# New keys for the attention units' schedule: scores in 0.95 of a unit, transposed scores in 0.9

## The chip, the core and the metric

The kernel runs on one core of one Trainium2 chip. The core's engines work side by side, each through its own instructions in a fixed order: TensorE (PE, matmuls; its weight loads are shown as PEld), VectorE (DVE), ScalarE (ACT), GpSimd (POOL), and SyncE (SP), which issues most DMAs. The metric is the device time of one execution in microseconds, as the median of several runs.

## The reference

One transformer block on 2048 rows of 576 columns. A condition vector gives six modulation vectors (shift, scale and gate for each half). The first half is attention in 32 heads of 18 columns with a sliding window of 256 keys:

```python
q, k, v = qkv[0], qkv[1], qkv[2]
scores = jnp.einsum("bhqd,bhkd->bhqk", q, k) * (Dh ** -0.5)
mask = (idx[:, None] - idx[None, :] >= 0) & (idx[:, None] - idx[None, :] < W)
scores = jnp.where(mask[None, None], scores, -1e9)
p = _softmax(scores, axis=-1)
o = jnp.einsum("bhqk,bhkd->bhqd", p, v)
...
x = x + ga * _A_ref(h, A_wqkv, A_wo)
h = _layernorm(x, axis=-1) * (1 + cb) + sb
x = x + gb * _B_ref(h, B_w1, B_w2, B_w3, B_w4)
```

The second half, `_B_ref`, mixes rows by small shifts and applies an MLP with 4608 inner columns. All of it is in float32; the kernel reaches that accuracy by splitting operands into an upper and a lower half and summing three products.

## The kernel before

The kernel has three stages. `phase_a` is attention with its projections, `phase_b` the row mixing, `phase_c` the MLP. The change lies in `phase_a` alone.

**Units.** Queries come in 4 groups of 512 rows, heads in 8 packs of 4. That gives 32 *units*, u = 0 to 31, each for four heads of one group. A unit's work, by the functions that the listing below shows:

- `pack(u)` (SP) loads the unit's queries and keys from DRAM into one of three buffers `Q[u % 3]`, `K[u % 3]`, as nine DMAs (L494 queries, L497 keys); they may start when the unit three back has used the buffer for the last time.
- `scores(u)`: 16 score matmuls (`one`, L511; four row tiles by four heads) go into a ring of three PSUM banks. VectorE adds the mask and reduces each to its row maxima (`red`, L518). After the sixteenth, `neg` (VectorE, L524 and L525, 16 columns each) negates the maxima in two halves, `mt` transposes them on TensorE (L532), `ms` copies them on ScalarE (L537) and issues a small DMA from ScalarE's queue (L538), which puts them as two extra rows into the unit's queries.
- `attend(u)`: 12 transposed scores (`xs`, three bank layouts by four heads, each some matmuls of L558 and mask matmuls of L567) go into a ring of two PSUM banks; because of the extra rows the maxima are subtracted already. ScalarE takes the exponential (`ex`, L577). Then `av` multiplies by the values (48 matmuls of L588, or fewer in the first group), `cp` copies the result, `ot` transposes it (L599), `on` divides by the sums, and `store` writes it to DRAM.

**Between the units** stand the projections: `qk_item` (queries and keys of a group, 14 matmuls of 512 columns in 7 steps, L417, then copy, split and store) and `v_item` (values, 288 columns in 4 steps). Ahead of each group from the second on, the group's four row tiles are normalised (`x_norm`) and transposed (`x_tr`): TensorE transposes column block k into the bank `tr` or `mm` (L381), ScalarE scales it (`ev`, L389), GpSimd casts the upper half (`hi`, L392), and VectorE subtracts for the lower half (`lo`, L396). GpSimd also sums the later modulation vectors (`modvec`, L649, L651) and scales the output weights (L698). From unit 22 on `s4a` applies the output projection to finished row tiles: it loads a tile's attention rows and x, transposes them (L888), multiplies (L922), and normalises twice; the loads and the weights for the next stage join SP's queue.

**The order** is written out by hand. Each step is a pair of a *key* and a function; the keys count in units. All pairs are sorted by key and the functions called in that order (`play`), so every engine gets its instructions in the order of the keys. At run time nothing is reordered: a key is no time, only a place. In a stretch where fewer matmuls have keys TensorE goes through the keys faster. An engine whose next instruction waits holds back all behind it.

In `s4a`, `quiet` moves a load or store whose key has a fraction between 0.04 and 0.38 to the fraction 0.38, and `free` chooses PSUM banks that the bank `av` of the units does not use at that time. The class constants `win` (the keys between which each group's projections run), `o_p`, `o_x` and `o_a` are offsets of the packing, the transposed scores and the attend matmuls.

Of the kernel before, what the change touches and what calls it, by code (L numbers as in the profile page):

```python
# [53 lines left out]
class Kern:  # L54
# [132 lines left out]
    def phase_a(self):  # L187
# [10 lines left out]
        with ExitStack() as st:  # L198
# [40 lines left out]
            def vones(a, b):  # L239
                def f():  # L240
                    for v in V[a:b]:
                        nc.gpsimd.memset(v, 1.0)
                return f
# [128 lines left out]
            def x_tr(g, k, t0):  # L372
                n = P if k < KC else TAIL
                box = {}

                def tr():
                    if k == 0:
                        hT[g] = gp.tile([P, 2 * KC + 1, 512], F32R, tag="L", name=f"hT{g}", bufs=1)
                    pa = box["p"] = ps([P, 4, P], ("tr", "mm", "tr", "mm", "tr")[k], f"hT{g}_{k}")
                    for i in range(4):  # L380
                        nc.tensor.transpose(pa[:n, i, :], xrows[4 * g + i][:, k * P:k * P + n], self.ident)  # L381

                def ev():
                    if k % 2 == 0:
                        h0["t"] = kp.tile([P, 2, 512], F32, tag="qe", name=f"h{g}_{k}", bufs=2)
                    h = h0["t"][:, k % 2, :]
                    box["h"] = h
                    p = h0["p"][k] if g == 0 else box["p"]
                    nc.scalar.activation(h[:n], p[:n].rearrange("p a b -> p (a b)"), AF.Identity, bias=sa[:n, k:k + 1], scale=ca[:n, k:k + 1])  # L389

                def hi():
                    nc.gpsimd.tensor_copy(hT[g][:n, k if k < KC else 2 * KC, :], box["h"][:n])  # L392

                def lo():
                    o = hT[g][:, KC + k, :] if k < KC else hT[g][TAIL:, 2 * KC, :]
                    nc.vector.tensor_tensor(out=o, in0=box["h"][:n], in1=hT[g][:n, k if k < KC else 2 * KC, :].bitcast(F32), op=ALU.subtract)  # L396
                if g == 0:
                    b = -8.84 + 0.01 * k if k < KC else -8.79
                    return [(b, ev), (b + 0.001, hi), (b + 0.021, lo)]
                return [(t0, tr), (t0 + 0.02, ev), (t0 + 0.055, hi), (t0 + 0.105, lo)]  # L400

            def x_tr0(i):
                def f():
# [96 lines left out]
            def scores(u):  # L500
                g = u // NU
                q, k = Q[u % 3], K[u % 3]
                box, reds = [], {}

                def one(i, h):
                    def f():
                        if not box:
                            box.append(sm.tile([P, 4, 4], F32, tag="m", name=f"m{u}", bufs=2))
                        lo = 0 if g else max(0, 2 - i) * P
                        sc = ps([P, 3 * P], "sc", f"sc{u}_{i}_{h}")  # L510
                        nc.tensor.matmul(sc[:, lo:], q[0:2 * R3, h, i * P:(i + 1) * P], k[0:2 * R3, h // 2, i * P + lo:(i + 3) * P], start=True, stop=True)  # L511
                        reds[i, h] = sc, lo
                    return f

                def red(i, h):
                    def f():
                        sc, lo = reds[i, h]
                        nc.vector.tensor_tensor_reduce(out=sc[:, lo:], in0=sc[:, lo:], in1=mask[:, lo:], scale=1.0, scalar=-3e38, op0=ALU.add, op1=ALU.max, accum_out=box[0][:, i, h:h + 1])  # L518
                    return f

                def neg():
                    m = box[0]
                    mr = sm.tile([P, 4, 8], F32R, tag="mr", name=f"mr{u}", bufs=2)
                    nc.vector.scalar_tensor_tensor(out=mr[:, :, 0:4], in0=m, scalar=-1.0, in1=zeros, op0=ALU.mult, op1=ALU.add)  # L524
                    nc.vector.scalar_tensor_tensor(out=mr[:, :, 4:8], in0=m, scalar=-1.0, in1=mr[:, :, 0:4].bitcast(F32), op0=ALU.mult, op1=ALU.subtract)  # L525
                    box.append(mr)

                def mt():
                    mr = box[1]
                    pm = ps([8, 4, P], "av" if 0 < u < 23 else "tr", f"mT{u}", F32R)  # L530
                    for i in range(4):
                        nc.tensor.transpose(pm[:, i, :], mr[:, i, :], self.identr)  # L532
                    box.append(pm)

                def ms():
                    ms = kp.tile([8, 512], F32R, tag="avs", name=f"ms{u}", bufs=1)
                    nc.scalar.copy(ms, box[2].rearrange("p a b -> p (a b)"))  # L537
                    nc.scalar.dma_start(q[2 * R3:2 * R3 + 2, :, :].bitcast(F32), ms.bitcast(F32))  # L538
                e = []
                for n, (i, h) in enumerate((i, h) for i in range(4) for h in range(4)):  # L540
                    t = u - 1 + (n + 0.5) / 16
                    e += [(t, one(i, h)), (t + 0.02, red(i, h))]
                return e + [(u + 0.01, neg), (u + 0.13, mt), (u + 0.15, ms)]

            banks = [[(0, 0, 3, 1), (3, 3, 1, 0)], [(1, 1, 3, 0), (-2, 0, 1, 3)], [(-1, 0, 2, 0), (2, 2, 2, 2)]]
            low = [((0, 3, 1), (1, 0, 2)), ((1, 0, 1), (0, 2, 2)), ((None, 1, 2),)]
# [1 line left out]
            def attend(u):  # L548
# [5 lines left out]
                def xs(b, h):  # L554
                    def f():
                        x = ps([P, 512], "st", f"X{u}_{b}_{h}")
                        for n, (kb, q0, w, p0) in enumerate(bk[b]):
                            nc.tensor.matmul(x[:, p0 * P:(p0 + w) * P], k[0:2 * R3 + 2, h // 2, (kb + 2) * P:(kb + 3) * P], q[0:2 * R3 + 2, h, q0 * P:(q0 + w) * P], start=(n == 0), stop=False)  # L558
                        c0 = min(s[3] for s in bk[b])
                        c1 = max(s[3] + s[2] for s in bk[b])  # L560
                        ms = []
                        for m, p0, w in low[b]:
                            p0, w = max(p0, c0), min(p0 + w, c1) - max(p0, c0)
                            if w > 0:
                                ms.append((maskb[:, 2 - w:2] if m is None else maskb[:, m].unsqueeze(1).to_broadcast([P, w, P]), p0, w))
                        for n, (m, p0, w) in enumerate(ms):
                            nc.tensor.matmul(x[:, p0 * P:(p0 + w) * P], self.identb, m, start=False, stop=(n == len(ms) - 1))  # L567
                        X[b, h] = x, c0, c1
                    return f
# [10 lines left out]
                def av(b):  # L580
                    def f():
                        if not abox:
                            abox.append(ps([P, 512], "av", f"av{u}"))
                        for n, (kb, q0, w, p0) in enumerate(bk[b]):
                            v = V[(4 * g + kb) % 10]
                            for h in range(4):
                                hh = 4 * (u % NU) + h
                                nc.tensor.matmul(abox[0][32 * h:32 * h + 32, q0 * P:(q0 + w) * P], v[:, hh * VA:hh * VA + 32], Pt[b, h // 2][:, p0:p0 + w, h % 2, :], start=(b == 0 and n == 0), stop=(b == 2 and n == len(bk[b]) - 1))  # L588
                    return f
# [34 lines left out]
                e = []  # L624
                for b in range(3):
                    for h in range(4):
                        t = u + self.o_x + (4 * b + h + 0.5) / 12
                        e += [(t, xs(b, h)), (t + 0.015, ex(b, h))]
                    e.append((u + self.o_x + 1 + self.o_a - 0.001 * (2 - b), av(b)))
                t = u + self.o_x + 1 + self.o_a  # L630
                return e + [(t + 0.03, cp), (t + 0.152, ot), (t + 0.167, on), (t + (0.36 if u < NB * NU - 1 else 0.17), store)]

            def modvec(v):
# [76 lines left out]
            ev = [(-9.5, warm(36)), (-9.45, consts), (-9.44, vones(0, 4)), (-9.405, c_load), (-9.2, wm_load), (-9.05, cond)]  # L710
# [6 lines left out]
            for k in range(KC + 1):  # L717
                ev += x_tr(0, k, 0.0)
# [21 lines left out]
            for g in range(1, NB):  # L740
# [11 lines left out]
                t = w0  # L752
# [21 lines left out]
            for t in range(12):  # L774
                t0 = w1 + 0.12 + 0.72 * t
# [79 lines left out]
        self.lc = itertools.count()  # L855

    win = {1: (2.6, 9.25), 2: (9.7, 16.1), 3: (16.55, 22.73)}
    o_p, o_x, o_a = 1.6, 0.42, 0.18

    def s4a(self, t, kp):  # L860
        nc, gp, Wo = self.nc, self.gp, self.Wo
        base = self.win[NB - 1][1] + 0.12 + 0.72 * t

        def free(a, b):
            lo, hi = self.o_x + self.o_a - 0.08, self.o_x + self.o_a + 0.04
            return all((base + a - n > hi) or (base + b - n < lo) for n in range(int(base), int(base) + 3))
        if free(0.56, 0.785):
            kinds = "mm", "av", "av" if free(0.135, 0.2) else "mm"
# [75 lines left out]
        e = [(quiet(-0.6, -0.25), load_o), (quiet(-0.35, 0.2), load_x)]  # L944
# [627 lines left out]
```

## Time and profile before

| what | value |
|---|---|
| median of 3 runs | 1675.13 us (1673.27 to 1676.79) |
| profiled execution | 1673.19 us |
| its span, first to last instruction | 1671.4 us |
| busy share of PE, DVE, ACT, POOL | 98%, 70%, 43%, 49% |
| mean granted TensorE clock | 0.998 |

How to read the lines that follow. In a *timeline* a line is start in us, duration in us, engine, source line, operation, output tile, inputs, shapes and a count; in brackets the engine's idle time just before it and whose end released it. PE's matmuls overlap, so a matmul's duration is longer than the time to the next one's start. In a *table of waits* a line is who waited, for whom, and total us, number of waits, longest us. In the *table by stage* a line is the stretch, its length, the busy time (and count) of PE, PEld, DVE, ACT and POOL, the granted clock, the DMA engines' share and GB/s. L with a number is a line of the kernel before.

### The profile page before, as it was taken

To read this page: it belongs to the slowest core of one execution; us is meant where nothing else is said; L and a number is where in the kernel's file an instruction comes from. 1 tells how busy PE (TensorE), PEld (TensorE's weight loads), DVE (VectorE), ACT (ScalarE), POOL (GpSimd) and SP (SyncE) were. 2 spreads that over 40 slices of the span, in tenths; PEclk is the share of its full clock that TensorE was granted. 3 is DMA by queue.
4 is the path that set the end of the run, shared out by engine and by line. 5 is a ranking of instruction groups with operands and counts; after the bars stand their busy time and mean duration, and the time that the engine had idled before them with its cause. 6 is when DMAs were issued, how large, how long until landed. Compare 5 with 4: busy or idle time off the path is not lost.

```text
span 1671.4 us, 30559 instructions
## 1 busy us (share of the span) xinstructions
PE 1638.5 (98%) x11115; PEld 1423.2 (85%) x11115; DVE 1163.4 (70%) x2417; ACT 714.7 (43%) x1373; POOL 816.0 (49%) x833
## 2 busy tenths in 40 slices
PE   9999999999999999999999999999999999999999
PEld 5877788778777787889999999999999999999998
DVE  5765765666666774767788878888885666666667
ACT  3454554555546656444344434443424222222221
POOL 6432332232436552243478888888863333322335
PEclk9999999999999999999999999999999999999999
DMA  7654554545477756345356556555575454445443
GB/s 227 192 152 133 147 145 133 151 110 153 118 170 210 216 181 200 124 137 189 123 211 222 197 172 216 206 200 177 214 246 179 152 168 158 134 144 176 148 133 109
DMA packets 160190, 283.03 MB, mean 169 GB/s; under 512 B 37412, under 2 KB 76836, under 8 KB 160040
## 3 DMA queue, kind: packets, MB, share of 16 engines
q1 hardware_dynamic: 159720, 280.55, 54.2%
q8 instruction: 88, 1.44, 0.4%
q14 instruction: 62, 0.51, 0.1%
q10 hardware_dynamic: 320, 0.52, 0.1%
HBM read 168.71 MB, written 111.63 MB: 168 GB/s over the span
## 4 chain that ended last, share of the span: by engine, by line
PE 88%; DVE 4%; DMA 2%; POOL 2%; ACT 2%; issue 2%; SPq 0%; ACTq 0%; POOLq 0%; DVEq 0%
PE pall L1431 27%; PE pall L1477 24%; PE pall L417 9%; PE pall L588 5%; PE pall L558 4%; PE pall L511 4%; PE pall L834 3%; PE pall L567 3%; PE pall L1213 3%; PE pall L922 2%; DVE pall L518 1%; PE pall L973 1%; PE pall L599 1%; DMA Q<-ms 1%; DMA wm<-in_w_mod_dram 1%
## 5 line engine op out<-in xcount | busy, mean ns | idle before, releaser
L1477 PEld LDWEIGHTS pall<-W,G 128*128 128x128 f32 x3036 | 428.3, 188 | 19.2
L1477 PE MATMUL pall<-W,G 128*128 128x288 f32 x3036 | 440.6, 294 | 0.0
L518 DVE CUSTOM_DVE_ANT_0 pall<-pall,mask 128x384 f32<-128x384 f32 (+2 forms) x512 | 270.3, 544 | 174.1 <-PE pall L511 171.5
L1431 PE MATMUL pall<-LNT,W 128*128 128x512 f32 x1512 | 374.8, 390 | 0.0
L1486 DVE TENSOR_TENSOR accA<-pall,accA 128x576 f32<-128x576 f32 (+1 forms) x337 | 254.0, 755 | 120.8 <-PE pall L1477 109.2
L1402 POOL TENSOR_TENSOR g<-g,g 128x512 f32<-128x512 f32 x140 | 185.3, 1324 | 292.7 <-DVE G L1397 150.4
L1431 PEld LDWEIGHTS pall<-LNT,W 128*128 128x128 f32 x1512 | 274.7, 188 | 45.5
L577 ACT ACTIVATE P<-pall 128x512 f32<-128x512 f32 (+2 forms) x384 | 216.8, 571 | 153.8 <-PE pall L567 145.2
L1394 ACT CAST G<-g 128x512 fp32r<-128x512 f32 x249 | 151.1, 620 | 271.6 <-POOL g L1402 270.4
L1397 DVE TENSOR_TENSOR G<-g,G 128x512 fp32r<-128x512 f32 x249 | 240.7, 968 | 11.6 <-ACT G L1394 11.5
L1435 ACT ACTIVATE g<-pall 128x512 f32<-128x512 f32 x144 | 85.8, 596 | 194.6 <-PE pall L1431 185.0
L1486 DVE TENSOR_TENSOR accB<-pall,accB 128x576 f32<-128x576 f32 x134 | 101.3, 757 | 91.1 <-PE pall L1477 89.2
L417 PE MATMUL pall<-hT,Wc 128*128 128x512 f32 x504 | 161.3, 420 | 3.2 <-ACT Wc L322 1.9
L511 PE MATMUL pall<-K,Q 108*128 108x384 f32 (+2 forms) x352 | 125.3, 367 | 1.5 <-DVE m L518 1.3
L1431 PE MATMUL pall<-big,W 128*128 128x512 f32 x504 | 126.2, 390 | 0.0
L442 POOL CAST qe<-qe 128x512 fp32r<-128x512 f32 x36 | 22.6, 627 | 211.1 <-ACT qe L438 184.3
L567 PE MATMUL pall<-maskb,identb 128*128 128x256 bf16 (+1 forms) x640 | 120.1, 253 | 0.0
L558 PE MATMUL pall<-Q,K 110*128 110x384 f32 (+1 forms) x480 | 104.5, 291 | 4.1 <-ACT P L577 3.1
L1431 PEld LDWEIGHTS pall<-big,W 128*128 128x128 f32 x504 | 90.9, 188 | 14.1
L417 PEld LDWEIGHTS pall<-hT,Wc 128*128 128x128 f32 x504 | 86.5, 193 | 16.7 <-issue 2.9
L558 PEld LDWEIGHTS pall<-Q,K 110*128 110x128 f32 x480 | 85.0, 190 | 17.4 <-issue 5.4
L588 PE MATMUL pall<-P,V 128*32 128x384 f32 (+2 forms) x1408 | 84.3, 386 | 0.7 <-DVE oT L909 0.6
(663 smaller groups left out, 2389.3 us busy)
## 6 DMA issues: line engine op xcount, KB each, us to landing
w4d<-W SPq DMA_DIRECT2D x55, 576.0 KB
W<-w4d SPq DMA_DIRECT2D x55, 576.0 KB
w3d<-W SPq DMA_DIRECT2D x36, 640.0 KB
W<-w3d SPq DMA_DIRECT2D x36, 640.0 KB
r<-in_B_w_dram SPq DMA_DIRECT2D x36, 288.0 KB
K<-k0d SPq DMA_DIRECT2D x32, 216.0 KB
Q<-q0d SPq DMA_DIRECT2D x88, 72.0 KB
wm<-in_w_mod_dram SPq DMA_DIRECT2D x17, 288.0 KB
```

What stands on the lines that cost most here:

```text
L417: nc.tensor.matmul(pm, pl()[i][0], pl()[i][1], start=(i == 0), stop=(i == 13))
L511: nc.tensor.matmul(sc[:, lo:], q[0:2 * R3, h, i * P:(i + 1) * P], k[0:2 * R3, h // 2, i * P + lo:(i + 3) * P], start=True, stop=True)
L518: nc.vector.tensor_tensor_reduce(out=sc[:, lo:], in0=sc[:, lo:], in1=mask[:, lo:], scale=1.0, scalar=-3e38, op0=ALU.add, op1=ALU.max, accu ...
L558: nc.tensor.matmul(x[:, p0 * P:(p0 + w) * P], k[0:2 * R3 + 2, h // 2, (kb + 2) * P:(kb + 3) * P], q[0:2 * R3 + 2, h, q0 * P:(q0 + w) * P], ...
L567: nc.tensor.matmul(x[:, p0 * P:(p0 + w) * P], self.identb, m, start=False, stop=(n == len(ms) - 1))
L577: nc.scalar.activation(pt[:, c0:c1, h % 2, :], x[:, c0 * P:c1 * P].rearrange("p (a b) -> p a b", b=P), AF.Exp, scale=SCALE)
L588: nc.tensor.matmul(abox[0][32 * h:32 * h + 32, q0 * P:(q0 + w) * P], v[:, hh * VA:hh * VA + 32], Pt[b, h // 2][:, p0:p0 + w, h % 2, :], st ...
L1397: nc.vector.tensor_tensor(out=sp[m][:, 1], in0=src(), in1=sp[m][:, 0].bitcast(F32), op=sub)
L1402: nc.gpsimd.tensor_tensor(out=g[o] if o in g else gt(o), in0=g[a], in1=g[b], op=op)
L1431: nc.tensor.matmul(box["p"], box["l"][i][1], box["l"][i][0], start=(i == 0), stop=(i == 13))
L1477: nc.tensor.matmul(po, a, b, start=(n == 0), stop=(n == len(seq) - 1))
L1486: nc.vector.tensor_tensor(out=ac, in0=po, in1=ac, op=ALU.add)
```

## The change

Only keys change; no instruction is added or removed.

- The 16 scores and reductions of a unit are spread over 0.95 of a unit instead of a whole one, from the same start.
- The negation's key goes from u + 0.01 to u - 0.03, that of the maxima's transposition from u + 0.13 to u + 0.12, that of their copy and DMA from u + 0.15 to u + 0.14.
- The 12 transposed scores start at u + 0.44 instead of u + 0.42 and are spread over 0.9 of a unit instead of a whole one. The attend matmuls and all behind them have u + 1.6 as before, now by a constant of their own, `o_v`; `free` is written with it and has the same bounds.
- The packing's key goes from u - 1.6 to u - 1.64.
- In `x_tr` the cast to the upper half goes from 0.055 to 0.06 behind the transposition, the subtraction for the lower half from 0.105 to 0.15.

```diff
-                return [(t0, tr), (t0 + 0.02, ev), (t0 + 0.055, hi), (t0 + 0.105, lo)]
+                return [(t0, tr), (t0 + 0.02, ev), (t0 + 0.06, hi), (t0 + 0.15, lo)]
...
-                    t = u - 1 + (n + 0.5) / 16
+                    t = u - 1 + 0.95 * (n + 0.5) / 16
                     e += [(t, one(i, h)), (t + 0.02, red(i, h))]
-                return e + [(u + 0.01, neg), (u + 0.13, mt), (u + 0.15, ms)]
+                return e + [(u - 0.03, neg), (u + 0.12, mt), (u + 0.14, ms)]
...
-                        t = u + self.o_x + (4 * b + h + 0.5) / 12
+                        t = u + self.o_x + 0.9 * (4 * b + h + 0.5) / 12
                         e += [(t, xs(b, h)), (t + 0.015, ex(b, h))]
-                    e.append((u + self.o_x + 1 + self.o_a - 0.001 * (2 - b), av(b)))
-                t = u + self.o_x + 1 + self.o_a
+                    e.append((u + self.o_v - 0.001 * (2 - b), av(b)))
+                t = u + self.o_v
...
-    o_p, o_x, o_a = 1.6, 0.42, 0.18
+    o_p, o_x, o_v = 1.64, 0.44, 1.6
...
-            lo, hi = self.o_x + self.o_a - 0.08, self.o_x + self.o_a + 0.04
+            lo, hi = self.o_v - 1.08, self.o_v - 0.96
```

## The prediction

> **What bounds the kernel now.** I read the page first, then the busy times by stage, then the waits inside the attention stage, and last the order of time around the longest of them.
>
> ```profile
> span 1671.4 us, 30559 instructions
> PE 1638.5 (98%) x11115; PEld 1423.2 (85%) x11115; DVE 1163.4 (70%) x2417; ACT 714.7 (43%) x1373; POOL 816.0 (49%) x833
> ```
> ```profile
> 57.00:670.00 613.00, 591.56 (x4908) 482.97 (x4908) 402.49 (x1328) 340.24 (x636) 227.59 (x296) 1.00 0.58 160
> ```
>
> The first columns of the stage's row are the stretch, its length and PE's busy time. TensorE (PE) bounds the kernel, here at full granted clock (1.00). The diff touches only the attention stage, 57 to 670 us, where PE is idle for 613.0 - 591.6 = 21.4 us. The change removes no work from PE, so all it can do is to shorten or lengthen these waits, about 1.3% of the time. The waits of this stretch (total, times, longest; PEld is PE's weight load, the first to wait):
>
> ```profile
> PEld pall L532 <- DVE mr L525: 7.1, 9, 1.6
> PEld pall L558 <- ACT P L577: 6.9, 10, 1.6
> PEld pall L511 <- DVE m L518: 5.9, 11, 1.3
> DVE hT L396 <- POOL hT L392: 5.1, 5, 1.9
> PEld pall L381 <- ACT h L389: 2.3, 4, 1.0
> ```
>
> First comes the transposition of the negated maxima (L532), late because of the negation on VectorE (L525); then the transposed scores (L558), which find their two banks still held by the exponentials; then the scores (L511), whose three banks are held by the reductions. One unit's turn, the worst:
>
> ```profile
> 431.38 0.34 PE L511 MATMUL pall<-K,Q 108*128 108x384 f32 x1
> 431.56 0.56 PE L417 MATMUL pall<-Wv,hT 128*128 128x288 f32 x3
> 431.95 0.34 PE L511 MATMUL pall<-K,Q 108*128 108x384 f32 x1
> 432.13 0.40 PE L558 MATMUL pall<-big 110*128 110x384 f32 x2
> 432.37 0.34 PE L567 MATMUL pall<-maskb,identb 128*128 128x128 bf16 x2
> 432.47 0.78 PE L417 MATMUL pall<-Wv,hT 128*128 128x288 f32 x4
> 433.08 0.34 PE L511 MATMUL pall<-K,Q 108*128 108x384 f32 x1
> 433.26 0.41 PE L558 MATMUL pall<-big 110*128 110x256 f32 x2
> 435.20 0.41 PE L532 MATMUL pall<-identr,mr 128*8 128x128 f32 x4 [1.42 <-DVE mr L525]
> ```
> ```profile
> 432.42 1.38 DVE L524 SCALAR_TENSOR_TENSOR mr<-m,zeros 128x16 fp32r<-128x16 f32 x1
> 433.83 1.32 DVE L525 SCALAR_TENSOR_TENSOR mr<-m,mr 128x16 fp32r<-128x16 f32 x1
> ```
> ```profile
> 432.34 1.42 POOL L651 TENSOR_TENSOR wm<-wm 128x576 f32<-128x576 f32 x1
> 433.72 2.77 POOL L698 TENSOR_TENSOR wor<-wor,ga 128x576 f32<-128x576 f32 x2
> ```
>
> The unit's last score starts at 431.38; one score and two matrix pieces and transposed scores later PE stands until the negation ends at 435.15. Two instructions on 16 columns took 2.7 us, each ending with a GpSimd product. From starts to the next start, PE's pieces cost: a score 0.18 (431.95 to 432.13), a transposed score 0.34 (432.13 to 432.47), four 288-wide matmuls 0.61.
>
> **The change, term by term.** All are keys of one list per engine, so I sorted both sets of keys for each engine. Work, engines and counts stay; GpSimd's order stays too.
>
> *Maxima's transposition.* The last score of unit u stood at u - 0.031 and comes to u - 0.080, its reduction at u - 0.060; the negation follows that reduction directly in both orders for all but one unit, so it gains no place on VectorE: its new key alone is worth nothing. What counts is PE's work between last score and transposition: keys 0.161 of a unit before, 0.200 after. In it lie two scores of the next unit as before, but three transposed scores instead of two (the earlier unit's ninth is at u + 0.078 and its seventh moves to u - 0.073). So nearly every unit gets 0.34 us more cover, units 20 and 21 (the worst above) also a matrix piece of four matmuls (0.95 in all), unit 16 two (1.2). The other waits on the negation:
>
> ```profile
> 107.45 0.41 PE L532 MATMUL pall<-identr,mr 128*8 128x128 f32 x4 [0.93 <-DVE mr L525]
> 124.61 0.40 PE L532 MATMUL pall<-identr,mr 128*8 128x128 f32 x4 [0.16 <-DVE mr L525]
> 173.94 0.41 PE L532 MATMUL pall<-identr,mr 128*8 128x128 f32 x4 [0.59 <-DVE mr L525]
> 339.61 0.41 PE L532 MATMUL pall<-identr,mr 128*8 128x128 f32 x4 [0.31 <-DVE mr L525]
> 473.88 0.40 PE L532 MATMUL pall<-identr,mr 128*8 128x128 f32 x4 [0.91 <-DVE mr L525]
> 568.90 0.40 PE L532 MATMUL pall<-identr,mr 128*8 128x128 f32 x4 [0.60 <-DVE mr L525]
> 626.58 0.41 PE L532 MATMUL pall<-identr,mr 128*8 128x128 f32 x4 [0.58 <-DVE mr L525]
> ```
>
> To each idle time belong 0.2 us more, which the modelled end of the matmul in front hides (7.1 us in 9 weight loads against 5.5 in these seven and the 1.42). Less the cover, in the order of the rows: 0.8, 0, 0.45, 0 (unit 16), 0.75, 0.45, 0.45, and 0.7 for the worst: 3.6 left. Term: 3.6 - 7.1 = **-3.5 us**; ends -7.1 (all gone) and 0 (the negations run into longer GpSimd work).
>
> What the negation meets is the open part. In the rows it ends with the GpSimd instruction beside it. [...]
>
> *The landing of the negated maxima.* The transposed scores of a unit start when its DMA of the maxima has landed. Its transposition comes 0.01 earlier and the first piece 0.016 later, with one more score (0.18) between.
>
> ```profile
> 60.14 0.50 PE L558 MATMUL pall<-Q,K 110*128 110x384 f32 x2 [0.32 <-DMA Q<-ms]
> 611.78 0.47 PE L558 MATMUL pall<-Q,K 110*128 110x384 f32 x2 [0.17 <-DMA Q<-ms]
> ```
>
> Four such waits, first and last shown, each lose about 0.15: **-0.6**; ends 0 and -1.5.
>
> *Exponentials.* A transposed score waits for the exponential two places back. Behind the transposition ScalarE must copy, issue a DMA and then do the tenth exponential, before the twelfth piece may start:
>
> ```profile
> 209.90 0.57 ACT L537 CAST ms<-pall 8x512 fp32r<-8x512 f32 x1
> 210.50 0.62 ACTq L538 DMA_DIRECT2D Q<-ms  x1
> 211.17 1.08 ACT L577 ACTIVATE P<-pall 128x512 f32<-128x512 f32 x2 [0.70 <-PE pall L511]
> ```
> ```profile
> 211.82 0.39 PE L558 MATMUL pall<-big 110*128 110x256 f32 x1 [0.75 <-ACT P L577]
> ```
>
> From 209.90 to 211.71 that is 1.8 us. PE's cover, transposition to twelfth piece, shrinks from 0.248 to 0.183 of a unit: beside the transposition itself 4 x 0.18 + 2 x 0.34 = 1.40 us becomes 1.22, and the matrix pieces in it, which lie in lumps, fall by some 0.4. With a matrix piece at 0.5, unit by unit, the sorted lists leave this cover short by 2.1 us in all before and by 4.7 after: +2.6. Three present waits have another cause:
>
> ```profile
> 534.00 0.50 PE L558 MATMUL pall<-Q,K 110*128 110x256 f32 x2 [1.29 <-ACT P L577]
> 554.52 0.50 PE L558 MATMUL pall<-Q,K 110*128 110x384 f32 x2 [0.34 <-ACT P L577]
> 575.21 0.50 PE L558 MATMUL pall<-Q,K 110*128 110x384 f32 x2 [1.27 <-ACT P L577]
> ```
>
> For the last, near key 28.44, the eleventh exponential comes to stand ahead of two normalisations that delayed it (-1.5 with the hidden 0.2), for the middle one the tenth ahead of a copy (-0.3). For the first, near 26.31, the ninth escapes two long pieces, but the copy of the maxima then stands behind them (+0.4). Term **+1.2**; ends -1.5 (these waits less, nothing new) and +8.9 (the shortfalls of the list and a piece of 0.5 more in a dozen units).
>
> *Scores in 0.95.* A score waits for the reduction three places back: 0.188 of a unit before, 0.178 after. Where transposed scores now pause (key 0.30 to 0.48) a score loses one or two of them as cover, 0.3 to 0.6 us; where scores pause (0.92 to 1.03) the next three gain 0.3 to 0.8. Over the places with waits or under 0.6 us to spare, losses come to 2.5 and gains to 2.3 us: **0**, ends -2.3 and +2.5.
>
> *The halves of x.* The upper half moves 0.005, the lower 0.045 of a unit ((626.58 - 107.45) / 28 = 18.5 us, so 0.8 us) on VectorE, behind one or two more reductions, so that it waits less for the cast (5.1 us in 5 above). PE pays for that in one score wait of 0.3. The transpositions of x (L381, 2.3 us) wait for ScalarE, which in this stretch has two exponentials fewer: -0.9. Term **-1.2**; ends 0 and -2.7. The first matmul that reads a lower half has key w0 + 0.067, the half w0 - 0.25; the tail's half w0 + 0.07 is read at w0 + 0.29. The cover is 0.22 of a unit, 4 us; without it the delay of 0.8 us in three groups would cost up to 2.5.
>
> *Packing.* Its loads go out 0.04 earlier, behind the earlier last use of Q and K, and pass on SP's queue a store of queries or, in seven units, tile loads and stores with key 0.38. Nine issues run from
>
> ```profile
> 323.53 1.54 SPq L494 DMA_DIRECT2D big<-q0d  x2
> 327.31 0.32 SPq L497 DMA_DIRECT2D big<-k1d  x1
> ```
>
> so those go out 4 us later. The chain in order of time shows a short landing:
>
> ```profile
> 57.50 2.60 DMA Q<-ms
> ```
>
> The tightest is the fifth tile's attention rows, read 0.35 of a unit (6.5 us) on; with such a landing hardly anything is left over. I take 0, upper end +2. The attend matmuls stay at u + 1.6 (0.42 + 1 + 0.18), as do the bank choices.
>
> **Sum.** -3.5 - 0.6 + 1.2 + 0 - 1.2 = -4.1 us. The profiled execution took 1673.2 us (span 1671.4 and 1.8 around), 1.9 under the median 1675.1; it becomes 1669.1, and the median 1671.0.
>
> **Rivals.** *More goes:* every wait on the negation vanishes and ScalarE adds none: -7.1 - 0.6 - 1.2 = -8.9, 1666.2 us. For it: the cover needed beyond 0.3 us is under a microsecond in each case. Against: the ScalarE shortfalls are worked out in the same way. Chance 0.17. *The products hit again:* negations meet other GpSimd products, as long as the 1.42 us above, and the first term is near 0: -0.6, 1674.5 us. For it: two instructions on 16 columns took 2.7 us beside such products. Against: GpSimd's order is untouched. Chance 0.25. *Slower, by ScalarE:* the copy and DMA of the maxima sit in front of the exponential that the twelfth piece needs, and other ScalarE work falls between. It decides from a ScalarE term of 8.7 on (0.24 us a unit more than I counted, over 31 units); at its end: -3.5 - 0.6 + 8.9 - 1.2 = +3.6, 1678.7 us. For it: by the lists the mean cover to spare falls from about 0.9 us to 0.3. Against: a pause of 0.175 follows in which ScalarE recovers. Chance 0.16.
>
> **Chances.** The forecast has 0.42; its own range is 1668 to 1673.5. Changes within 0.2% (3.35 us) can hardly be told from none here. Faster: 0.35 of the forecast, 0.17 and 0.03 of the second rival, together 0.55; slower: 0.14 of the last; the rest, 0.31, within. The range reaches from just below the first rival to just short of the last one's: 1664.5 to 1677.5.
>
> **What would show it.** Right: waits of L532 on L525 at 4 us or less, waits on DMA Q<-ms gone, waits of L558 on L577 a little up and gathered at the twelfth piece, L396 waiting less for L392, PE idle from 57 to 670 near 17 us. Wrong: L532 waits kept with L524 and L525 as long as now, or L558 waits doubled; a wait of L888 on a load would show the packing's price.

## The result and the profile after

The changed kernel takes 1681.08 us (median of 12 runs, 1678.37 to 1684.42) against 1675.03 us of the kernel before (12 runs, 1673.27 to 1680.26) beside it: a ratio of 1.0032, 95% interval 1.0022 to 1.0042. It is slower by some 5 to 6 us, where 4.1 us less were predicted.

The page of the changed kernel:

```profile
span 1677.5 us, 30555 instructions
PE 1643.2 (98%) x11115; PEld 1424.5 (85%) x11115; DVE 1163.8 (69%) x2417; ACT 716.7 (43%) x1373; POOL 818.5 (49%) x833
```

The span grew by 6.1 us, as the medians did, and PE shows 4.7 us more busy time for the same 11115 matmuls. Two stretches lost the time: the last attend matmul (L588) starts at 652.0 us before and 655.0 after (+3.0), and the first matmul of the MLP (L1431) at 808.2 and 814.4 (+6.1). From there on the traces run parallel. So half of the loss lies in the attention stage and half in the row mixing, whose keys did not change.

The attention stage's waits after, with the same columns as before (for whom, total, times, longest). PEld rows first, then four of PE and VectorE:

```profile
PEld pall L558 <- ACT P L577: 12.0, 19, 2.2
PEld pall L511 <- DVE m L518: 5.0, 11, 1.1
PEld pall L381 <- ACT h L389: 4.2, 7, 1.1
PEld pall L532 <- DVE mr L525: 2.1, 5, 0.8
PE pall L888 <- DMA s4rows<-od: 1.8, 1, 1.8
PE pall L888 <- DMA or<-od: 1.2, 1, 1.2
PE pall L558 <- DMA Q<-ms: 0.3, 1, 0.3
DVE hT L396 <- POOL hT L392: 2.5, 5, 0.8
```

The wait for the negation (L532) fell from 7.1 to 2.1 us and the waits for the landing of the maxima went from four to one, as forecast. But the transposed scores' wait for ScalarE (L558) rose from 6.9 to 12.0, that of the transpositions of x (L381) from 2.3 to 4.2, and the output projection (L888) now waits twice for its attention rows, 3.0 us in all. PE is idle for 20.7 us of the stretch from 57 to 670 us, where the prediction's sign of being right was about 17.

**The negation.** The worst unit of the prediction (L524 and L525 took 1.38 and 1.32 us, 1.42 us of idle time), in the changed kernel, as a timeline:

```profile
433.80 0.27 DVE L524 SCALAR_TENSOR_TENSOR mr<-m,zeros 128x16 fp32r<-128x16 f32 x1
434.11 0.68 DVE L525 SCALAR_TENSOR_TENSOR mr<-m,mr 128x16 fp32r<-128x16 f32 x1
...
435.95 0.40 PE L532 MATMUL pall<-identr,mr 128*8 128x128 f32 x4
```
```profile
434.02 0.75 POOL L649 TENSOR_SCALAR wm<-wm,silu 128x576 f32<-128x576 f32 x1
434.86 1.43 POOL L651 TENSOR_TENSOR wm<-wm 128x576 f32<-128x576 f32 x1
```

The two instructions take 0.95 us instead of 2.70 and end at 434.79, 1.2 us ahead of the transposition. They now lie beside a shorter GpSimd instruction, L649 (L525 took 0.68 us beside its 0.75, where before L524 took 1.38 beside the 1.42 of L651), and are done before L651 starts. So in this unit the wait went further than by the cover that the prediction counted, and that was luck of the place.

**The exponentials.** One of the new waits, unit 6, on PE and on ScalarE:

```profile
158.12 0.40 PE L532 MATMUL pall<-identr,mr 128*8 128x128 f32 x4
...
160.50 0.38 PE L558 MATMUL pall<-big 110*128 110x256 f32 x1 [0.69 <-ACT P L577]
```
```profile
158.79 0.58 ACT L537 CAST ms<-pall 8x512 fp32r<-8x512 f32 x1
159.39 0.62 ACTq L538 DMA_DIRECT2D Q<-ms  x1
160.06 0.66 ACT L577 ACTIVATE P<-pall 128x256 f32<-128x256 f32 x2 [0.70 <-PE pall L511]
```

This is the mechanism that the prediction gave: copy, DMA issue, tenth exponential, and only then the twelfth piece. PE came to the twelfth piece 1.7 us after the transposition and waited. From start to start of PE's matmuls, the lost time at L558 for ScalarE is 5.3 us before and 9.0 after; 4.8 of the 9.0 lie in eight units at this piece (key u + 0.30), against 1.7 in two of them before. Besides these, the place near key 26.3 grew: 1.29 us idle before, at the eleventh piece, and after, at the twelfth,

```profile
538.31 0.50 PE L558 MATMUL pall<-Q,K 110*128 110x256 f32 x2 [1.95 <-ACT P L577]
```
```profile
535.63 0.57 ACT L537 CAST ms<-pall 8x512 fp32r<-8x512 f32 x1
536.24 0.62 ACTq L538 DMA_DIRECT2D big<-ms  x1
536.90 0.87 ACT L155 ACTIVATE s4rows<-s4rows,b3rs 128x576 f32<-128x576 f32 x1 [0.70 <-DVE s4rows L927]
537.68 1.06 ACT L577 ACTIVATE P<-pall 128x512 f32<-128x512 f32 x2
```

**The packing.** The fifth tile's attention rows (L879), SP's issues and PE's first transposition of them. Before:

```profile
511.58 0.45 SPq L879 DMA_DIRECT2D s4rows<-od  x1
...
512.87 3.23 SPq L494 DMA_DIRECT2D Q<-q0d  x2
```
```profile
523.32 0.60 PE L888 MATMUL pall<-ident,s4rows 128*128 128x128 f32 x4
```

After:

```profile
514.10 1.41 SPq L494 DMA_DIRECT2D Q<-q0d  x2
...
517.75 0.32 SPq L497 DMA_DIRECT2D K<-k1d  x1
518.17 0.35 SPq L943 DMA_DIRECT2D hbd<-s4rows  x1
519.27 0.35 SPq L943 DMA_DIRECT2D xp<-s4rows  x1
519.68 0.44 SPq L879 DMA_DIRECT2D s4rows<-od  x1
```
```profile
526.38 0.65 PE L888 MATMUL pall<-ident,s4rows 128*128 128x128 f32 x4 [1.80 <-DMA s4rows<-od]
```

Before, the load went out ahead of the nine packing DMAs and had 11.7 us. After, it went out behind them, 8.1 us later, and its landing released PE 6.7 us after its issue (526.38 - 519.68); 4.9 us had passed when PE stood. The semaphore updates in the traces give the landing of this same load in other kernels: 4.9 us after its issue before, 3.9 and 3.4 in the first two kernels below, where it goes out ahead of the packing again, and 6.8 in the third, where it goes out behind. So this load took 3.4 to 4.9 us to land ahead of the packing, and 6.7 and 6.8 behind it; what holds it up there is not shown.

**The row mixing.** DVE's and PE's rows of the changed kernel where its first new wait lies:

```profile
682.66 0.82 DVE L987 SCALAR_TENSOR_TENSOR s4rows<-s4rows,b13mv,cbB 128x576 f32<-128x576 f32 x1 [1.61 <-DMA xp<-s4rows]
...
683.90 1.90 PEld L973 LDWEIGHTS pall<-Wo,oT 128*128 128x128 f32 x14 [1.33 <-DVE s4rows L974]
```

VectorE waits for a store to have read its tile, and PE for VectorE: 1.3 us, which the profile of before does not have. The rest of the 3.1 us is put down to the granted clock, shown at the end.

### The profile page after: what moved, and what is told of

It is laid out like the page before. It is cut to its first block, busy times and chain, and to the rows that moved or that the text cites. A ratio compares the mean times of both kernels' runs of the same rounds, so it can differ in the third digit from the quotient of the medians.

```text
span 1677.5 us, 30555 instructions
## 1 busy us (share of the span) xinstructions
PE 1643.2 (98%) x11115; PEld 1424.5 (85%) x11115; DVE 1163.8 (69%) x2417; ACT 716.7 (43%) x1373; POOL 818.5 (49%) x833
## 4 chain that ended last, share of the span: by engine, by line
PE 89%; DMA 3%; ACT 3%; DVE 2%; issue 1%; POOL 1%; SPq 0%; ACTq 0%; POOLq 0%; DVEq 0%
PE pall L1431 27%; PE pall L1477 24%; PE pall L417 10%; PE pall L511 4%; PE pall L588 4%; PE pall L558 4%; PE pall L834 3%; PE pall L567 3%; PE pall L1213 3%; PE pall L922 2%; DVE pall L518 1%; PE pall L599 1%; ACT P L577 1%; PE pall L973 1%; DMA wm<-in_w_mod_dram 1%
## 5 line engine op out<-in xcount | busy, mean ns | idle before, releaser
L1431 PE MATMUL pall<-LNT,W 128*128 128x512 f32 x1512 | 374.8, 390 | 0.0
L1431 PEld LDWEIGHTS pall<-LNT,W 128*128 128x128 f32 x1512 | 274.8, 188 | 45.4
L511 PE MATMUL pall<-K,Q 108*128 108x384 f32 (+2 forms) x352 | 126.9, 371 | 2.0 <-DVE m L518 1.2
L1431 PE MATMUL pall<-big,W 128*128 128x512 f32 x504 | 126.2, 390 | 0.0
L558 PE MATMUL pall<-Q,K 110*128 110x384 f32 (+1 forms) x480 | 105.7, 294 | 4.9 <-ACT P L577 4.4
L1431 PEld LDWEIGHTS pall<-big,W 128*128 128x128 f32 x504 | 90.9, 188 | 14.1
L558 PEld LDWEIGHTS pall<-Q,K 110*128 110x128 f32 x480 | 85.2, 191 | 15.0 <-ACT P L577 8.5
L588 PE MATMUL pall<-P,V 128*32 128x384 f32 (+2 forms) x1408 | 84.3, 386 | 1.1 <-DVE oT L909 1.1
```

Source lines behind the costliest of these rows:

```text
L1431: nc.tensor.matmul(box["p"], box["l"][i][1], box["l"][i][0], start=(i == 0), stop=(i == 13))
```

## The experiments

Three causes were weighed: the loads that stand behind the packing on SP's queue; the transposed scores squeezed into 0.9 of a unit, so that PE comes to them before ScalarE is done; and the maxima's copy, which the nearer key puts ahead of one more exponential. Each kernel was timed beside the kernel before, and its ratio is to that one.

**The packing's key back.** The changed kernel with

```diff
-    o_p, o_x, o_v = 1.64, 0.44, 1.6
+    o_p, o_x, o_v = 1.6, 0.44, 1.6
```

> The changed kernel with one constant put back: the packing's key is u - 1.6 again instead of u - 1.64; all else stays changed. Theory A, the packing: in the trace of the changed kernel two transpositions of attention rows (L888) wait 1.2 and 1.8 us for their loads, which now go out behind the packing's nine DMAs, and right after the second wait the granted clock is at half for 3.4 us (worth 1.7 us). With the old key the loads go out first: both waits and that stretch of half clock go, some 4.7 us, about 1676.4 us. Theory B, ScalarE: the waits of the transposed scores for exponentials (6.9 us before, 12.0 after) and of the transpositions of x (2.3 and 4.2) made the loss; the packing is hidden as the prediction had it: no change, 1680 to 1682 us.

1677.37 us, 1.0010 (1.0001 to 1.0020). This one key is worth 0.0022, 3.7 us of the changed kernel's loss. No wait of L888 on a load is left; L558 stays at 12.9 us.

**The same without moving the packing.** In the changed kernel `quiet` puts the loads at fraction 0.34 instead of 0.38, so that they go out ahead of the packing, which keeps u - 1.64:

```diff
-            d = a if not 0.04 < f < 0.38 else a + 0.38 - f
+            d = a if not 0.04 < f < 0.34 else a + 0.34 - f
```

> The changed kernel with the tile loads and stores of the output projection moved, not the packing: those with a fraction from 0.04 go to 0.34 instead of 0.38, so ahead of the packing's new key 0.36. Theory A: as good as the packing put back, 1676 to 1677 us, no wait of L888 on a load. If it is the packing's own earlier start that hurts and not the loads behind it: stays near 1681. Theory B: no change, 1680 to 1682 us.

1676.7 us, 1.0002 (0.9992 to 1.0011). The loss goes again, and it is the order against the loads that counts, not the earlier packing.

**The loads put behind the packing in the kernel before:**

```diff
-            d = a if not 0.04 < f < 0.38 else a + 0.38 - f
+            d = a if not 0.04 < f < 0.42 else a + 0.42 - f
```

> The kernel before with the loads' order alone changed: the tile loads and stores with a fraction from 0.04 go to 0.42, so behind the packing at 0.40. Theory A: waits of L888 on loads appear as in the changed kernel, and 3 to 5 us are lost, 1678 to 1680 us. Theory B: no change, 1674 to 1676 us.

1681.77 us, 1.0036 (1.0024 to 1.0048). With every other key as before, this order (and the 0.04 of a unit by which the loads are later) costs 6 us. The fifth tile's row in this kernel:

```profile
527.29 0.65 PE L888 MATMUL pall<-ident,s4rows 128*128 128x128 f32 x4 [2.93 <-DMA s4rows<-od]
```

So the packing's term, which the prediction took as 0 with an upper end of 2 us, is shown to be about 4 to 6 us (3.7, 5.0 and 6.0 by the three ratios).

**Transposed scores and packing back, the rest kept.** The changed kernel with

```diff
-                        t = u + self.o_x + 0.9 * (4 * b + h + 0.5) / 12
+                        t = u + self.o_x + (4 * b + h + 0.5) / 12
...
-    o_p, o_x, o_v = 1.64, 0.44, 1.6
+    o_p, o_x, o_v = 1.6, 0.42, 1.6
```

> The changed kernel with the transposed scores back at u + 0.42 over a whole unit, and with them the packing at u - 1.6 (it must stay behind the last use of the buffers): only scores, maxima and halves of x stay changed. Theory A alone: the same as with the packing put back, about 1676.4 us. Theory B alone: the loss of 5 to 7 us goes with the transposed scores, 1674 to 1676 us. Both: A's 4.7 us and B's 5 to 7 us go, 1669 to 1671 us; the waits of L532 on L525 rise again from 2.1 us to some 3 to 5, since there are two transposed scores in that stretch again instead of three.

1675.35 us, 0.9999 (0.9990 to 1.0008), and not the 1669 to 1671 us of both causes together. The squeeze is not the whole of ScalarE's loss: without it the waits (PEld) are still

```profile
PEld pall L558 <- ACT P L577: 10.3, 15, 2.7
PEld pall L532 <- DVE mr L525: 5.1, 9, 1.1
```

**The squeeze alone, in the kernel before:**

```diff
-                        t = u + self.o_x + (4 * b + h + 0.5) / 12
+                        t = u + self.o_x + 0.9 * (4 * b + h + 0.5) / 12
...
-    o_p, o_x, o_a = 1.6, 0.42, 0.18
+    o_p, o_x, o_a = 1.6, 0.44, 0.16
```

> The kernel before with the transposed scores alone changed (u + 0.44, 0.9 of a unit; attend matmuls at u + 1.6 and packing at u - 1.6 as before). If squeezing them makes ScalarE late: waits of L558 on L577 rise from 6.9 to 10 us or more, those of L532 on L525 stay near 7, and it is 3 to 5 us slower, 1679 us. If ScalarE's loss comes only from the copy of the maxima standing at u + 0.14: waits of L558 stay near 7 and the time near 1675.

1681.01 us, 1.0037 (1.0025 to 1.0050). Alone it costs as much as the whole change:

```profile
PEld pall L558 <- ACT P L577: 10.8, 17, 2.7
PEld pall L532 <- DVE mr L525: 8.1, 13, 1.7
PEld pall L511 <- DVE m L518: 7.2, 14, 1.0
```

Against before, L558 lost 3.9 us more, L532 1.0 and L511 1.3. On top of the other parts the same edit costs less (the fourth kernel here against the first: 0.9999 to 1.0010), since there L558 waits 10.3 us already. The parts do not add.

**The old keys for the maxima.** The fourth kernel with their transposition and copy as before:

```diff
-                return e + [(u - 0.03, neg), (u + 0.12, mt), (u + 0.14, ms)]
+                return e + [(u - 0.03, neg), (u + 0.13, mt), (u + 0.15, ms)]
```

> The run with the transposed scores put back, with the maxima's transposition and copy at their old keys too (u + 0.13, u + 0.15), so that the copy and its DMA stand behind the ninth exponential (u + 0.143) again and not ahead of it. Scores in 0.95, negation at u - 0.03 and the halves of x stay changed. Theory C: at u + 0.14 the copy holds up the ninth exponential, and that took back what the negation's wait gave; then L558's waits fall from 10.3 to about 7 us, L532's stay at 5 or below, 3 us faster than that run: 1672 us. Rival, the gain is taken by something else (clock, landings): no better than 1675.

1672.6 us, 0.9989 (0.9980 to 0.9998). Hundredths of a unit decide over the waits: at u + 0.14 the copy stood ahead of the ninth exponential (u + 0.143), at u + 0.15 behind it, and L558 waits 6.9 us instead of 10.3. The time is 0.0010 lower, which is no more than the uncertainty. The waits now:

```profile
PEld pall L558 <- ACT P L577: 6.9, 9, 1.8
PEld pall L532 <- DVE mr L525: 1.9, 4, 0.9
```

The nearer transposition itself took cover from the negation (L532 5.1 against 1.9 us).

**The copy behind the tenth exponential.** The second kernel here (changed, loads first) with

```diff
-                return e + [(u - 0.03, neg), (u + 0.12, mt), (u + 0.14, ms)]
+                return e + [(u - 0.03, neg), (u + 0.15, mt), (u + 0.1685, ms)]
```

> The changed kernel with the loads first (0.34), and the maxima's transposition at u + 0.15 and their copy at u + 0.1685 instead of 0.12 and 0.14: behind the tenth exponential (u + 0.1675), which the twelfth transposed score waits for. Theory C: L558's waits on L577 fall from 12.4 to about 6 us, L532's from 2.9 to about 1; waits on the DMA of the maxima rise by 1 us. Some 6 us faster than that run: about 1670.5 us, faster than both kernels. Rival: ScalarE is late for its other work, not for its place: L558's waits stay above 10 us, 1675 to 1677 us.

1683.49 us, 1.0053 (1.0040 to 1.0065), a miss.

```profile
PEld pall L511 <- DVE m L518: 7.0, 12, 1.2
PEld pall L558 <- ACT P L577: 6.4, 11, 1.6
PEld pall L381 <- ACT h L389: 5.9, 7, 1.4
PEld pall L417 <- ACT V L480: 4.9, 6, 1.8
PEld pall L417 <- ACT qe L438: 3.6, 6, 1.2
```

L558's waits go from 12.4 to 6.4 us as meant, but PE then stands for other work of ScalarE and for the reductions. A wait was moved, not removed.

**The halves of x alone, in the kernel before:**

```diff
-                return [(t0, tr), (t0 + 0.02, ev), (t0 + 0.055, hi), (t0 + 0.105, lo)]
+                return [(t0, tr), (t0 + 0.02, ev), (t0 + 0.06, hi), (t0 + 0.15, lo)]
```

> The kernel before with the halves of x alone later (0.06 and 0.15). The prediction's term: -0.3 us by fewer waits of VectorE on the cast (L396 on L392, 5.1 us), and a gain of 0.9 us at L381 that belongs to the transposed scores' pause and not to this edit; so 1674.5 to 1675.5 us, no difference that can be measured. Rival: the lower half is late for the projection's matmuls (L417 waits on L396): 1676 us or more.

1674.47 us, 0.9997 (0.9988 to 1.0005): no difference that can be told from none.

**Scores and negation alone, in the kernel before:**

```diff
-                    t = u - 1 + (n + 0.5) / 16
+                    t = u - 1 + 0.95 * (n + 0.5) / 16
...
-                return e + [(u + 0.01, neg), (u + 0.13, mt), (u + 0.15, ms)]
+                return e + [(u - 0.03, neg), (u + 0.13, mt), (u + 0.15, ms)]
```

> The kernel before with the scores in 0.95 of a unit and the negation at u - 0.03 alone; copy and transposition of the maxima, transposed scores, packing and halves of x as before. If the prediction's first term holds by itself, waits of L532 on the negation fall from 7.1 to 1.5 to 2.5 us, those of L558 stay near 7, and the median is 1672 to 1673.5, as in the kernel that has the halves of x beside it. Rival: that kernel's gain came with the halves of x out of the negation's way on VectorE; then L532 stays above 4 us and the median is 1674.5 or more.

1672.51 us, 0.9979 (0.9970 to 0.9988), the lowest ratio here, and faster than both kernels of the change.

```profile
PEld pall L558 <- ACT P L577: 6.6, 9, 1.8
PEld pall L511 <- DVE m L518: 5.4, 10, 1.4
PEld pall L532 <- DVE mr L525: 1.6, 4, 0.9
```

**Further the same way.** The sixth kernel with scores in 0.9 of a unit and the negation at u - 0.08:

```diff
-                    t = u - 1 + 0.95 * (n + 0.5) / 16
+                    t = u - 1 + 0.9 * (n + 0.5) / 16
...
-                return e + [(u - 0.03, neg), (u + 0.13, mt), (u + 0.15, ms)]
+                return e + [(u - 0.08, neg), (u + 0.13, mt), (u + 0.15, ms)]
```

> The best kernel so far (scores in 0.95, negation at u - 0.03, halves of x later, all else as before; 1672.6) with scores in 0.9 of a unit and the negation at u - 0.08. If cover for the negation is all that counts, the last 1.9 us of L532 go to under 1, and the median is 1671 to 1672.5. Rival: the scores then wait for the reductions three places back, now 0.169 of a unit against 0.178; L511 grows from 5.1 us to 8 or more, and the median is 1674 to 1677.

1674.11 us, 0.9991 (0.9982 to 1.0000): no better than the sixth kernel's 0.9989.

```profile
PEld pall L558 <- ACT P L577: 8.9, 13, 2.5
PEld pall L511 <- DVE m L518: 7.3, 16, 1.0
PEld pall L532 <- DVE mr L525: 0.7, 1, 0.7
```

Against the sixth kernel L532 lost 1.2 us less, and L558 and L511 4.2 us more.

**The parts in a row.** These kernels are a ladder, each with one edit more than the one above:

| kernel | ratio to before | 95% interval |
|---|---|---|
| scores in 0.95, negation at u - 0.03 | 0.9979 | 0.9970 to 0.9988 |
| + halves of x later | 0.9989 | 0.9980 to 0.9998 |
| + maxima's transposition and copy nearer | 0.9999 | 0.9990 to 1.0008 |
| + transposed scores in 0.9 from u + 0.44 | 1.0010 | 1.0001 to 1.0020 |
| + packing at u - 1.64 (the change) | 1.0032 | 1.0022 to 1.0042 |

The first step is clear of 1, and the last is clear of the row above it. Each of the three between is about as large as its uncertainty; together (0.9979 to 1.0010, 5 us) they are not. By these ratios one part gains 3.5 us (2.8 by the medians) and the others give back 9. Since the parts do not add, a step's share holds for this order of steps.

## Why the prediction was wrong

**The step that failed most: packing at 0.** The prediction saw that the loads would go behind nine packing DMAs, named the fifth tile as the tightest, and then took the landing from a row of 2.60 us, that of the maxima: a DMA of eight rows on ScalarE's queue, which from 40 us on had issued nothing ahead of it. The load of 288 KB behind nine loads and two stores took 6.7 us, and the twelve loads of its kind (L879) in the profile of before took 3.1 to 7.7 us by their semaphores: none was as short as 2.60. The issue moved by 8.1 us and not by the 4 us taken, as SP was 2.1 us later ahead of the packing and then waited 1.9 us for its buffers. The prediction had 6.5 - 4 = 2.5 us left for the landing; the trace left 4.9. So there was more cover than it counted, and the landing was still 1.8 us too long for it. The wait of L888 on a load, which the prediction named as its sign, is there.

**Exponentials: mechanism right, size wrong.** The term was +1.2. The waits rose by 5.1 us in the table, 3.7 from start to start. The three places singled out came as worked out: from start to start they lost 3.5 us together before and 2.2 after (-1.3 against -1.4 forecast), the last and the middle one gone and the one near 26.3 grown. At the twelfth piece of the other units the lists were nearly right: 2.1 us before and 4.7 after were worked out, 1.7 and 4.8 are there. What the term left out are the other pieces: about 2 us are lost at fourth, sixth, eighth and ninth pieces, where before and the fourth kernel, without the squeeze, lose nearly nothing. The squeeze alone (the fifth kernel) loses time at the same pieces. So the step that failed here is that the closer spacing was priced at the tightest piece and at three old waits, and at nothing elsewhere. Unit 26 also meets a normalisation between the copy and the exponential. The nearer copy hurts L558 as well where the ninth exponential has its old key (6.9 and 10.3 us); in the change itself that exponential moves ahead of it, to u + 0.093, and the tenth, at u + 0.168, stands behind the copy with either key.

**Halves of x, -1.2: wrong in sign where it counted.** L396 waits less for the cast (5.1 to 2.5 us), as forecast, and alone the edit is worth nothing measurable. The 0.9 us at L381 did not come: those waits rose by 1.9 us with the squeeze (2.4 in the kernel with the transposed scores back, 4.2 in the one with them squeezed), which fits a ScalarE that is later there, not freer; that cause is argued, not shown.

**Maxima's transposition, -3.5: right, and somewhat more** (-5.0 in the change, -5.5 with the scores alone, where the median falls 2.8 us). The count of transposed scores between last score and transposition, on which the term rests, orders all twelve profiles: with two of them L532 waits 5.1 to 8.1 us for the negation (before and the third, fourth, fifth and eighth kernels), with three 1.1 to 2.9, with four (the last kernel) 0.7. The negations ran beside shorter GpSimd work in the worst unit, not longer. The landing of the maxima (-0.6) came as forecast: four waits, 1.0 us on PE, became one of 0.3. Scores in 0.95 (0) is near: L511 -0.9.

**Not in the prediction at all: the row mixing, +3.1 us.** Nothing in that stage is edited, and it was taken as fixed. 1.3 us is the wait of L973 behind a store; in seven of the ten other kernels it is 0.9 to 1.6 us too, the one with the halves of x alone among them, and in the one with the scores alone it is absent; why the store is late stays open. The other 1.7 is put down to the clock, by what is left and not by a test: the kernels with the wait and no dip of the clock in this stage took 1.1 to 2.3 us longer there than before, those with the dip and no wait 0.5 to 1.7.

Of the rivals, "slower by ScalarE" had the direction and the mechanism, but its condition, a ScalarE term of 8.7, was not met: it took the packing and the row mixing beside a term of 4 to 5. The waits that changed in the attention stage do not sum to its +3.0 us exactly, since a wait of a weight load is partly covered by the matmuls still running (L532 before: 7.1 us on PEld, 5.5 on PE).

## What to carry to other kernels

Take the landing of a load from a row with the same size and the same queue ahead of it, and not from the shortest on the page; where a move puts a load behind a burst of others, count the burst into the landing (here 6.7 us behind the nine packing DMAs, 4.9 ahead of them, and 2.60 for the maxima). Where a few hundredths in a key change which of two instructions goes first on a busy engine, sort the lists and price the pairs that swap; where pieces move closer together, price all of them and not only the tightest, which left out 2 us here. A bundle of edits is worth taking apart: here one part carried all of the gain, and the others together gave back more than it.

## What the hardware showed unexpectedly

The granted clock fell to half for 3.4 us after a stretch in which PE was not idle but about half busy (1.52 of 3.41 us and 1.72 of 3.40). By stage (stretch, length, PE, PEld, DVE, ACT, POOL, clock, DMA share, GB/s), the changed kernel around the packing's wait and in the row mixing:

```profile
524.28:527.69 3.41, 1.52 (x12) 1.02 (x10) 1.07 (x6) 1.18 (x2) 0.00 (x0) 1.00 0.86 308
527.69:531.10 3.41, 3.39 (x16) 3.07 (x17) 2.71 (x9) 0.97 (x2) 1.90 (x2) 0.51 1.03 283
...
753.00:756.40 3.40, 1.72 (x13) 1.11 (x12) 2.49 (x7) 0.35 (x2) 2.62 (x4) 1.00 0.72 224
756.40:759.80 3.40, 3.40 (x17) 3.38 (x17) 2.27 (x6) 0.65 (x2) 3.28 (x4) 0.50 0.32 117
```

Each such dip costs an estimated 1.7 us (half of 3.41). In the changed kernel's clock records the two start at 527.74 and 756.43 us, 522.24 and 750.93 us after the first record at 5.50: 153 and 220 times 3.413. In the twelve profiles of this case, from 40 to 800 us, I laid windows of that length, counted from the first record, over PE's busy time. All five that were under 0.45 busy were followed by a half-clock window; of thirteen between 0.49 and 0.54 eight were; of those above 0.55 none. In the changed kernel the window of the packing's wait (idle 1.80 us) was 0.44 busy, with a dip behind it, and the one from 534.56 us, with 1.61 of the 1.95 us of the longer wait ahead of 538.31, was 0.53 busy, with none. Before had no dip in that stretch of its profile (its emptiest window, from 432.43 us, is 0.58 busy), the changed kernel had two: by the estimate, 3.4 of the 6.1 us between the profiles. The dip near 750 us stands in six of the twelve, in the fastest kernel's too (748.55 to 751.96 us at 0.50, behind a window in which PE was busy for 1.72 of 3.41 us), so it isn't the mark of one edit. The mean granted clock is on record for the runs without a profile too: 0.9962 over the changed kernel's 12 runs, 0.9977 over 71 runs of the kernel before. A dip takes an estimated 0.001 off the mean (1.7 of 1675 us), so the changed kernel has about 1.5 more of them in a run, an estimate of 2.5 of its 5 to 6 us. Over the 177 runs with a clock on record, 0.001 less within a kernel's runs goes with 1.4 us more, which fits 1.7 for a dip.
